# Attention and adapters on one core: the first q's path, the last batch's parts, PSUM at the end, the load depth and the engine of the relus

## The chip, the core and the metric

The kernel runs on one core of a Trainium2 chip. The metric is the device time of one execution in microseconds (us). Before the change, 13 executions took 198.45 to 203.11 us, with a median of 201.2 us.

Five engines of the core work side by side, each through its own instructions in order: TensorE (PE; its weight loads are shown apart as PEld), VectorE (DVE), ScalarE (ACT), GpSimd (POOL) and SyncE (SP). Here POOL issues the loads that change the type on the way, SP issues the rest. Matrix products land in PSUM, which has 8 banks of 512 f32 per partition; DVE and ACT bring them from there to SBUF.

## What is computed

```python
# q, k, v: (8, 12, 448, 64) f32; w_gate (768, 8); A (8, 768, 16); B (8, 16, 768)
scores = scale * np.matmul(q, k.transpose(0, 1, 3, 2))
attn = np.maximum(scores, 0.0) ** 2 / S
attn_out = np.matmul(attn, v)
x = attn_out.transpose(0, 2, 1, 3).reshape(B * S, H * D)      # 3584 x 768
logits = x @ w_gate
topk = np.argpartition(-logits, K, axis=1)[:, :K]             # K = 2 of 8 experts
w = softmax over the two chosen logits
out = x + sum over the two: w * ((x @ A[e]) @ B[e])
```

## The kernel before

**Attention.** A quad is four heads of one batch (two heads in each half of the 128 partitions); with three quads a batch there are 24 quads. Per quad, three loads (q, k, v, line 305) of two DMAs each are issued on POOL and change f32 to bf16. PE transposes q and k (56 products, line 397) into two PSUM banks, and DVE copies all of it to `qkT` (line 408). A step `n` is 64 keys (`j`, seven of them) against a part of the batch's queries: four 64x64 products give the scores in two PSUM banks (`qk`, line 427), ACT takes the relu with a scale into the tile `a1` (line 450), DVE squares two steps at a time into `a2` (line 464), and PE multiplies by v, accumulating over the seven `j` (`pv`, line 481). The result goes to the transposed activations `xt` by one ACT and one DVE copy (`xt_copy`, line 504). In seven batches a step has all 448 queries; the last batch is worked in two parts of 224 (`UB = [1] * (B - 1) + [2]`), so that there are 147 steps of 448 and 42 of 224.

**Adapters.** Tokens go in 28 tiles of 128 columns of `xt`, and gates in groups of up to three tiles (the last two groups have two). `gate` multiplies by `awg`, the adapters' A and the gate weights side by side (line 522), picks the two experts in a chain of small DVE and ACT operations (lines 539 to 579), and transposes the weighted result (line 599) to `zT` (line 611). `outputs` adds, for each tile, x itself by products with the identity (`f_id`, line 628) and two f32 products with B (`f_b`, line 644) in two PSUM banks, copied to `osb` by ACT (one half) and DVE (the other, line 663) and stored from SP (line 679) in pieces of neighbouring rows of the output. `awg` itself is put in order by 72 products (line 345).

**The order of the work** is made on the host, before the launch, by a list scheduler (`schedule`, line 56): each operation has the engines that may take it, an assumed duration and latency, dependences, a rank (its due step, plus a constant `D_...` for its kind), and what it takes of pools and PSUM banks. On each engine the runnable operation of the lowest rank goes next; on PE a change of mode adds `SWITCH` to the rank, and a `qk` is put ahead when the relus that ACT still has to do would run out (`cover`, line 116). `choose` (line 79) grants PSUM: up to three pairs of banks for scores (`SCAP`), one tile for outputs at a time (`"o": 1`), and at most two of the four pairs for anything but scores. The order that comes out is what each engine's queue then holds. A load of quad x + `AHEAD` becomes runnable when quad x has been transposed; the first `AHEAD` quads' loads are issued at the start, after the identity, in the order q, k, v, with `sel` and A behind the first three quads (lines 685 to 695). `pv` of a first `j` waits for the squares `DEFER` steps later.

Of the kernel before, what the change touches and what calls it, by code (L numbers as in the profile page):

```python
# [14 lines left out]
J = 7  # L15
PH = 64
PU = 32

SLACK = -0.162
SWITCH = 1.913  # L20
THIRD = 0.612
SCAP, MCAP, TCAP = 3, 2, 1
DEFER = 5
AHEAD = 5
# [31 lines left out]
def schedule(ops, switch=0.1, hop=0.05):  # L56
# [8 lines left out]
    relus = []  # L65
    seq = {id(o): i for i, o in enumerate(ops)}
# [12 lines left out]
    def choose(o):  # L79

        c, n = o.want
        if used[c] >= {"s": SCAP, "t": TCAP, "p": 2, "m": MCAP, "o": 1}[c]:
            return None
        slots = sorted((x for x in range(0, 8, 2) if x in freed and x + 1 in freed),
                       key=lambda x: max(freed[x], freed[x + 1]))
        if c == "s":
            if used["s"] >= 2 and any(
                x.want and x.kind != "qk" and x.ready <= t + 1e-9 and x.rank <= o.rank + THIRD
                for x in avail["PE"]
            ):  # L90
                return None
            return [slots[0], slots[0] + 1] if slots else None
        halves = sorted((x for x in freed if x ^ 1 not in freed), key=lambda x: freed[x])
        if n == 1 and halves:
            return halves[:1]
        busy = 4 - len(slots) - used["s"]
        if not slots or busy >= 2:
            return None

        if n == 1 and busy == 1 and any(  # L100
            x.want and x.ready <= t + 1e-9 and x.kind in ("pv", "tp") and x.rank <= o.rank
            for x in avail["PE"]
        ):
            return None
        return [slots[0], slots[0] + 1][:n]

    def pick(e):
        c = [o for o in avail[e] if can(o)]
        if not c:
            return None  # L110
        if e != "PE":
            return min(c, key=lambda o: (o.rank, seq[id(o)]))
        best = min(c, key=lambda o: (o.rank + SWITCH * (o.mode != mode), seq[id(o)]))
        if best.kind != "qk":

            cover = max(free["ACT"], t) + sum(o.dur["ACT"] for o in relus)
            q = [o for o in c if o.kind == "qk"]
            if q and t + best.dur[e] + 0.1 * (best.mode != mode) + 0.1 * (best.mode != "64") + 0.4 > cover + SLACK:
                return q[0]
        return best  # L120

    left = len(ops)
    while left:
# [9 lines left out]
        for e in free:  # L133
# [42 lines left out]
            events.append(free[e])  # L176
            order.append(o)
# [18 lines left out]
def kernel(  # L196
# [51 lines left out]
    UB = [1] * (B - 1) + [2]  # L248

    D_QK = -3.314  # L250
    D_SQ = 6.0
    D_PV = 1.585
    D_XT = 3.031
    D_TP = -12.164
    D_TPE = -1.578
    D_Z = 0.984
    D_GATE = -2.244
    D_ZT = 12.0
    D_ZTE = 5.985
    D_ID = 9.569  # L260
    D_OUT = 13.172
# [3 lines left out]

    make_identity(nc, identf)
    nc.vector.tensor_copy(identb, identf)
# [23 lines left out]
    RELU = {448: 0.80, 224: 0.424}  # L291

# [7 lines left out]
    def load(b, w, c, deps):  # L300
        def fn():
            nm = f"{'qkv'[w]}n{c}"
            T[b, w, c] = loads.tile([128, 2, J * Dh], BF16, name=f"{nm}_{b}", tag=nm)
            for g in range(2):
                nc.gpsimd.dma_start(  # L305
                    out=T[b, w, c][g * PH : g * PH + PH],
                    in_=(qv, kv, vv)[w][b, g, :, 2 * c : 2 * c + 2, :],
                )


        return op(("POOL",), 1.3, 2.0, fn, deps=deps, kind="load")
# [24 lines left out]
    def aw_place(half, deps):  # L336

        d0 = half * 3

        def mm():  # L340
            for x in range(3):
                for i in range(DO):
                    y0 = 128 * (d0 + x) - i + DO - 1
                    for rhs, lo, hi in ((a_raw[:, :, i, :], 0, RE), (g_raw[:, i, :], RE, ZW)):
                        nc.tensor.matmul(  # L345
                            out=bank(m)[:, x * ZW + lo : x * ZW + hi],
                            lhsT=sel[:, y0 : y0 + 128],
                            rhs=rhs,
                            start=(i == 0 and lo == 0),
                            stop=(i == DO - 1),  # L350
                            skip_group_check=True,
                        )

        def ev():
            nc.vector.tensor_copy(
                awg[:, d0 : d0 + 3, :], bank(m)[:, : 3 * ZW].rearrange("p (x w) -> p x w", x=3)
            )

        m = op(PE, 18 * 0.085, PL, mm, deps=deps, mode="128", kind="fill", banks=("m", 1))
        return op(DVE, dve(3 * ZW), DL, ev, deps=[m], free=[(m, 0)], rank=-20.0)  # L360


    def width(b):
        return S // UB[b]

    order = []
    for b in range(B):
        if UB[b] == 1:
            order += [(b, 0, c, j) for c in range(NC_) for j in range(J)]
        else:  # L370
            order += [(b, u, c, j) for u in range(UB[b]) for c in range(NC_) for j in range(J)]
# [8 lines left out]
    while n < NS:  # L380
        m = 2 if n + 1 < NS and width(order[n][0]) == width(order[n + 1][0]) else 1
        for i in range(m):
            pair_of[n + i] = (n, m, i)
        n += m

    loaded, tp_ops = {}, {}
    qk_ops, relu_ops, sq_ops, pv_ops, xt_ops = {}, {}, {}, {}, {}

    def tp(b, c):
# [16 lines left out]
        def ev():  # L406
# [6 lines left out]
        m = op(PE, 2 * TPD, PL, mm, deps=[loaded[b, 0, c], loaded[b, 1, c]], mode="64", kind="tp",  # L413
               banks=("t", 2), take=("qkT",), rank=first_use[b, c] + D_TP)
        return op(DVE, dve(4 * J * PH, 1.92), DL, ev, deps=[m], free=[(m, 0)], rank=m.rank + D_TPE)

    def qk(n):
        b, u, c, j = order[n]
        pu = PH // UB[b]

        def fn():
            qk_ = T["qkT", b, c]
            for sl in range(2):
                r0 = sl * PH
                x0 = 0 if sl else 512 - width(b)
                for a in range(2):
                    nc.tensor.matmul(  # L427
                        out=bank(o, sl)[a * PH : a * PH + PH, x0 : x0 + width(b)].rearrange(
                            "p (j s) -> p j s", j=J
                        ),  # L430
                        lhsT=qk_[r0 : r0 + PH, a, 1, j * PH : j * PH + PH],
                        rhs=qk_[r0 : r0 + PH, a, 0, :].rearrange("p (j s) -> p j s", j=J)[
                            :, :, u * pu : u * pu + pu
                        ],
                        start=True,
                        stop=True,
                    )

        o = op(PE, 0.194 / UB[b], PL, fn, mode="64", kind="qk", deps=[tp_ops[b, c]],
               after=qk_ops.get(n - 1), banks=("s", 2), give=("qkT",) if n == last_use[b, c] else (), rank=n + D_QK)  # L440
        return o

    def relu(n):
        W = width(order[n][0])
        g0, m, i = pair_of[n]

        def fn():
            if i == 0:
                new("a1", ("a1", g0), [128, m, 2 * W], BF16)
            nc.scalar.activation(T["a1", g0][:, i], both(qk_ops[n], W), ACTF.Relu, scale=relu_scale)  # L450

        return op(ACT, RELU[W], AL, fn, deps=[qk_ops[n]], after=relu_ops.get(n - 1), kind="relu",
                  take=("a1",) if i == 0 else (), free=[(qk_ops[n], 0)], rank=n)

    def sq(n):

        W = width(order[n][0])
# [13 lines left out]
    def pv(n):  # L471
        b, u, c, j = order[n]
        W = width(b)
# [16 lines left out]
        if j == 0:  # L490
            wait += [sq_ops[min(n + DEFER, NS - 1)]]
        o = op(PE, 0.194 / UB[b], PL, fn, mode="64", kind="pv", deps=wait, after=pv_ops.get(n - 1),
               banks=("p", 2) if j == 0 else None, give=("a2",) if i == m - 1 else (),
               rank=n - j + DEFER + D_PV)
# [3 lines left out]
    def xt_copy(n):  # L498
        b, u, c, j = order[n]
        W = width(b)  # L500
        col = b * S + u * W
# [10 lines left out]
    def gate(tiles_):  # L512
        v = tile_due[tiles_[0]]
# [103 lines left out]
    def outputs(tile_):  # L617
# [52 lines left out]
        def st():  # L670
            osb = T["osb", tile_]
            r = 0
            while r < 128:
                b, x = divmod(c0 + r, S)
                pu = PH // UB[b]
                u, y = divmod(x, J * pu)
                j, p = divmod(y, pu)
                m = min(pu - p, 128 - r)
                nc.sync.dma_start(out=outv[b, j, u * pu + p : u * pu + p + m], in_=osb[r : r + m, :])
# [4 lines left out]

    b_load = op(("SP",), 0.5, 3.0, b_fn, kind="load")
    op(("POOL",), 1.4, 0.0, lambda: None)
    def first_loads(x0, x1):
        for x in range(x0, x1):
            for w in range(3):
                loaded[x // NC_, w, x % NC_] = load(x // NC_, w, x % NC_, [])  # L690

    first_loads(0, NC_)
    sel_op = op(("POOL",), 1.5, 0.1, sel_fn)
    a_load = op(("POOL",), 2.0, 3.0, aw_fn, kind="load")
    first_loads(NC_, AHEAD)
# [10 lines left out]
    for tl in range(NT):  # L706
        x = 128 * tl + 127
        b2, y = divmod(x, S)
        own = max(n for n, (b, u, c, j) in enumerate(order) if b == b2 and u == y // width(b)) + DEFER + 2
        tile_due[tl] = max(own, tile_due.get(tl - 1, 0) + PACE)  # L710
# [4 lines left out]
    def finish(n):  # L715
# [6 lines left out]
        for tl in range(NT):  # L722
# [3 lines left out]
            for col in range(128 * tl, 128 * tl + 128, PU):  # L726
                b2, x = divmod(col, S)
                need |= {(b2, x // width(b2), c2) for c2 in range(NC_)}
# [59 lines left out]
```

## Time and profile before

| | |
|---|---|
| median of 13 executions | 201.2 us |
| the profiled execution's own time | 201.77 us |
| its span, first to last instruction | 199.9 us |
| mean granted TensorE clock | 0.988 |
| first products of scores; first relu | 9.45 us; 10.09 us |
| last relu begins; last product ends; last copy ends | 181.04; 195.1; 195.70 us |
| last load issue on POOL | 116.4 us |

The profile gives busy times by engine, by 40 slices of the span, and by groups of instructions (line, engine, operation, tiles and shapes, with the mean duration of one, and what ended the idle time before them). A trace answers further: a table of busy time in chosen stretches, the instructions of a stretch in order of time (start, duration, engine, line, what it writes and reads, how many), and the chain of waits, followed back from the last instruction. Products are pipelined, so that one that stands alone shows more time than its place in a dense row.

### The profile page before, as it was taken

The page shows a single profiled execution, that of the slowest core. Times are in us where ns is not written, and L with a number is a line of the kernel's source. Part 1 is how long each engine was busy: PE and PEld are TensorE (multiplying, and loading weights), DVE is VectorE, ACT ScalarE, POOL GpSimd, SP SyncE. Part 2 cuts the span into 40 slices and gives each one's busy share as a digit, 9 for nine tenths or more (in the row PEclk, how much of TensorE's full clock was granted, in tenths as well). Part 3 has the DMA queues.
Part 4 walks back from the last instruction along what each step waited for, and adds up shares of the span by engine and source line. Part 5 has one row for each costly group of instructions (what it writes and reads, how often), then busy time and mean ns, then how long its engine had stood idle before and what let it go on. Part 6 is the DMA issues. An engine that isn't in the chain of part 4 may idle for free.

```text
span 199.9 us, 8860 instructions
## 1 busy us (share of the span) xinstructions
PE 172.9 (87%) x3908; PEld 102.7 (51%) x3908; DVE 161.2 (81%) x285; ACT 166.7 (83%) x255; POOL 89.3 (45%) x154
## 2 busy tenths in 40 slices
PE   0498878868999998999589998999998999999990
PEld 0345756545464555456346554565544756655640
DVE  0269879999799889998499999999999887895521
ACT  2099988999999989999599999999998799794220
POOL 8999899896967784977442720000000000000000
PEclk9999996999999999999999999999999999999998
DMA  5999999999999999999969892312330333336676
GB/s 114 173 183 142 168 168 183 192 179 172 155 220 234 218 187 201 198 209 202 194 126 164 122 194 62 77 27 65 79 82 3 82 84 82 82 79 150 161 178 151
DMA packets 26694, 28.70 MB, mean 144 GB/s; under 512 B 4512, under 2 KB 22944, under 8 KB 26656
## 3 DMA queue, kind: packets, MB, share of 16 engines
q0 software_dynamic: 21920, 16.73, 58.7%
q1 hardware_dynamic: 4736, 11.41, 20.8%
q8 instruction: 30, 0.49, 1.0%
q14 instruction: 8, 0.07, 0.1%
HBM read 33.84 MB, written 11.01 MB: 224 GB/s over the span
## 4 chain that ended last, share of the span: by engine, by line
PE 55%; ACT 21%; DVE 12%; issue 6%; DMA 2%; POOL 1%; ACTq 0%; DVEq 0%; POOLq 0%
PE ps L644 19%; ACT a L450 18%; PE ps L481 13%; PE ps L427 11%; DVE qkT L408 5%; PE ps L397 4%; DVE a L464 4%; PE ps L628 3%; PE ps L522 3%; DMA kn<-in_k_dram 2%; ACT xt L504 2%; PE ps L345 2%; DVE osb L663 1%; POOL qn L305 1%; PE ps L599 0%
## 5 line engine op out<-in xcount | busy, mean ns | idle before, releaser
L450 ACT ACTIVATE a<-ps 128x896 bf16<-128x896 f32 (+1 forms) x189 | 148.1, 863 | 14.9 <-PE ps L427 14.2
L464 DVE TENSOR_TENSOR a<-a 128x1792 bf16<-128x1792 bf16 (+1 forms) x95 | 92.0, 980 | 8.6 <-ACT a L450 8.2
L427 PE MATMUL ps<-qkT 64*64 64x448 bf16 (+1 forms) x756 | 64.2, 353 | 7.0 <-ACT a L450 4.6
L644 PE MATMUL ps<-B_sb,zT 128*128 128x384 f32 x112 | 49.2, 532 | 0.4 <-DVE zT L611 0.4
L481 PE MATMUL ps<-a,vn 64*64 64x448 bf16 (+1 forms) x756 | 45.4, 339 | 2.7 <-ACT a L450 1.7
L427 PEld LDWEIGHTS <-qkT 64*64 64x64 bf16 x756 | 24.0, 107 | 40.5 <-issue 33.4
L408 DVE COPY qkT<-ps 128x1792 bf16<-128x1792 bf16 x24 | 26.1, 1089 | 13.0 <-PE ps L397 12.5
L305 POOL DMA_DIRECT2D vn<-in_v_dram x48 | 29.3, 630 | 14.5 <-PE ps L427 6.9
L305 POOL DMA_DIRECT2D kn<-in_k_dram x48 | 29.5, 633 | 6.8 <-DMA qn<-in_q_dram 4.1
L481 PEld LDWEIGHTS <-vn 64*64 64x64 bf16 x756 | 25.2, 108 | 13.9 <-issue 7.6
L305 POOL DMA_DIRECT2D qn<-in_q_dram x48 | 29.4, 631 | 5.1 <-DMA vn<-in_v_dram 4.6
L663 DVE COPY osb<-ps 128x384 f32<-128x384 f32 x28 | 15.5, 553 | 9.3 <-PE ps L644 9.2
L663 ACT COPY osb<-ps 128x384 f32<-128x384 f32 x28 | 14.3, 510 | 9.5 <-PE ps L644 7.2
L644 PEld LDWEIGHTS ps<-B_sb,zT 128*128 128x128 f32 x112 | 17.2, 188 | 7.9 <-issue 4.0
L397 PE MATMUL ps<-identb,qn 64*64 64x64 bf16 x672 | 10.6, 201 | 6.7 <-DMA qn<-in_q_dram 6.1
L397 PEld LDWEIGHTS <-qn 64*64 64x64 bf16 x672 | 10.3, 116 | 10.6 <-DMA qn<-in_q_dram 6.3
L504 DVE CAST xt<-ps 128x448 bf16<-128x448 f32 (+1 forms) x27 | 15.3, 567 | 0.5 <-PE ps L481 0.5
L397 PE MATMUL ps<-identb,kn 64*64 64x64 bf16 x672 | 12.1, 203 | 3.7 <-issue 3.3
L504 ACT CAST xt<-ps 128x448 bf16<-128x448 f32 (+1 forms) x27 | 13.8, 511 | 1.7 <-PE ps L481 1.7
L522 PE MATMUL ps<-awg,xt 128*128 128x136 bf16 x168 | 13.7, 224 | 0.5 <-DVE qkT L408 0.5
L522 PEld LDWEIGHTS <-xt 128*128 128x128 bf16 x168 | 10.2, 98 | 5.6 <-issue 5.0
L628 PEld LDWEIGHTS <-xt 64*64 64x64 bf16 x672 | 10.0, 108 | 5.3 <-issue 3.9
(30 smaller groups left out, 71.8 us busy)
## 6 DMA issues: line engine op xcount, KB each, us to landing
out_dram<-osb SPq DMA_DIRECT2D x49, 192.0 KB, 3.5
qn<-in_q_dram POOLq DMA_DIRECT2D x48, 112.0 KB, 4.9
kn<-in_k_dram POOLq DMA_DIRECT2D x48, 112.0 KB, 5.1
vn<-in_v_dram POOLq DMA_DIRECT2D x48, 112.0 KB, 4.8
out_dram<-osb SPq DMA_DIRECT2D x14, 96.0 KB, 1.9
B_sb<-in_moe_B_dram SPq DMA_DIRECT2D x1, 384.0 KB, 3.2
a_raw<-in_moe_A_dram POOLq DMA_DIRECT2D x1, 192.0 KB, 4.0
g_raw<-in_moe_w_gate_dram POOLq DMA_DIRECT2D x1, 12.0 KB, 3.3
```

Of the source, the lines that this page charges most:

```text
L305: nc.gpsimd.dma_start(out=T[b, w, c][g * PH : g * PH + PH], in_=(qv, kv, vv)[w][b, g, :, 2 * c : 2 * c + 2, :],)
L397: nc.tensor.transpose(ps_b[sl * PH : sl * PH + PH, m.banks[g], (w * J + j) * PH : (w * J + j) * PH + PH,], T[b, w, c][r, sl, j * Dh : j * ...
L408: nc.vector.tensor_copy(sb.rearrange("p g w x -> p g (w x)"), ps_b[:, m.banks[0] : m.banks[0] + 2, : 2 * J * PH],)
L427: nc.tensor.matmul(out=bank(o, sl)[a * PH : a * PH + PH, x0 : x0 + width(b)].rearrange("p (j s) -> p j s", j=J), lhsT=qk_[r0 : r0 + PH, a, ...
L450: nc.scalar.activation(T["a1", g0][:, i], both(qk_ops[n], W), ACTF.Relu, scale=relu_scale)
L464: nc.vector.tensor_mul(a2, T["a1", g0], T["a1", g0])
L481: nc.tensor.matmul(out=bank(head, g)[sl * PH : sl * PH + PH, :W], lhsT=vn[r0 : r0 + PH, sl, j * Dh : j * Dh + Dh], rhs=T["a2", g0][r0 : r0 ...
L504: evac(W, lambda cp, g=g: cp(xt[:, g * NC_ + c, col : col + W], bank(src, g)[:, :W]), engs=SETS[(E_X0, E_X1)[g]], deps=[pv_ops[n]], free=[ ...
L522: nc.tensor.matmul(out=z[:, t * ZW : t * ZW + ZW], lhsT=xt[:, do, 128 * tiles_[t] : 128 * tiles_[t] + 128], rhs=awg[:, do, :], start=(do = ...
L628: nc.tensor.matmul(out=bank(o_id, r)[tok * PH : tok * PH + PH, do * PH : do * PH + PH], lhsT=xt[rr, do, c0 + tok * PH : c0 + tok * PH + PH ...
L644: nc.tensor.matmul(out=bank(o_id, r)[:, : D // 2].rearrange("p (o d) -> p o d", o=DO), lhsT=T["zT", g0][:, zi * 128 : zi * 128 + 128], rhs ...
L663: cp(T["osb", tile_].rearrange("p (o r d) -> p r o d", r=2, d=PH)[:, r], bank(o_id, r)[:, : D // 2].rearrange("p (o d) -> p o d", o=DO),)
```

## The change

It has eight parts.

1. The first quad's q is loaded by two plain f32 DMAs, one from SP and one from ACT, into an own tile, and turned to bf16 by one cast on DVE and one on ACT (`load_q0`). On SP it goes ahead of B.
2. The first load on POOL is then k of quad 0, ahead of the identity, which becomes a scheduled operation; then q, k of quad 1, v of quad 0, and so on. `sel` and A stand behind the loads of the first three quads but one v.
3. The first quad's transposes are copied in three: q by DVE, the first 64 keys by ACT, the other keys by DVE. The first `qk` needs the first two only.
4. Relus may go to DVE (`RDN = 189`: all steps). DVE takes one only if ACT is busy for more than `BEHIND` = 0.596 us yet, and after its own work whose rank is less than the relu's plus `YIELD` = 2.
5. The last batch has parts of 46 and 18 of each 64 rows: 322 and 126 queries, 21 steps each. The last part's columns run in the order of the output's rows, so that its store is one DMA.
6. PSUM: outputs may hold two tiles (`OCAP`), and three once no `qk` is left, when all four pairs may be used by others than scores.
7. `AHEAD` goes from 5 to 3, `DEFER` from 5 to 4; the assumed time of a load on POOL from 1.3 to 1.55.
8. All rank constants change (`SWITCH` from 1.913 to 5.491 among them); the last `pv`s and the last gate are ranked earlier by `HURRY` = 4.782; the products of line 345 come in six pieces instead of two, with a rank of their own (`D_A` = 18).

```diff
-SLACK = -0.162
-SWITCH = 1.913
-THIRD = 0.612
+SLACK = -0.248
+SWITCH = 5.491
+RDN = 189
+BEHIND = 0.596
+YIELD = 2.0
+OCAP = 2
+THIRD = 6.193
-DEFER = 5
-AHEAD = 5
+DEFER = 4
+AHEAD = 3
...
-        if used[c] >= {"s": SCAP, "t": TCAP, "p": 2, "m": MCAP, "o": 1}[c]:
+        if used[c] >= {"s": SCAP, "t": TCAP, "p": 2, "m": MCAP, "o": OCAP if qks else 3}[c]:
...
-        if not slots or busy >= 2:
+        if not slots or busy >= (2 if qks else 4):
...
+        if e == "DVE":
+            r = [o for o in c if o.kind == "relu"]
+            if r and free["ACT"] <= t + BEHIND:
+                c = [o for o in c if o.kind != "relu"]
+            elif r:
+                c = [o for o in c if o.kind == "relu" or o.rank < r[0].rank + YIELD]
...
-            return min(c, key=lambda o: (o.rank, seq[id(o)]))
+            return min(c, key=lambda o: (o.kind == "relu" and e == "DVE", o.rank, seq[id(o)]))
...
-    UB = [1] * (B - 1) + [2]
+    PARTS = [[(0, PH)]] * (B - 1) + [[(0, 46), (46, PH)]]
...
-    make_identity(nc, identf)
-    nc.vector.tensor_copy(identb, identf)
...
+    def load_q0():
+        def fn():
+            T["q0"] = const.tile([128, 2, J * Dh], F32, name="q0")
+            for g, e in enumerate((nc.sync, nc.scalar)):
+                e.dma_start(out=T["q0"][g * PH : g * PH + PH], in_=qv[0, g, :, 0:2, :])
+        def cast(sl):
...
+            (nc.vector.tensor_copy, nc.scalar.copy)[sl](T[0, 0, 0][:, sl], T["q0"][:, sl])
...
+        if first:
+            oq = op(DVE, dve(2 * J * PH, 1.92), DL, lambda: part(nc.vector.tensor_copy, 0, 0, J * PH),
+                    deps=[m], rank=-30.0)
+            ok = op(ACT, act(2 * PH), AL, lambda: part(nc.scalar.copy, 1, 0, PH), deps=[m], rank=-30.0)
+            o = op(DVE, dve(2 * (J - 1) * PH, 1.92), DL, lambda: part(nc.vector.tensor_copy, 1, PH, J * PH),
+                   deps=[oq], free=[(m, 0)], rank=-30.0)
...
-            nc.scalar.activation(T["a1", g0][:, i], both(qk_ops[n], W), ACTF.Relu, scale=relu_scale)
...
+            if o.eng == "ACT":
+                nc.scalar.activation(T["a1", g0][:, i], both(qk_ops[n], W), ACTF.Relu, scale=relu_scale)
+            else:
+                nc.vector.tensor_scalar(
+                    T["a1", g0][:, i], both(qk_ops[n], W), relu_scale, 0.0, op0=ALU.mult, op1=ALU.max
+                )
...
+                b, u, y = part_at(c0 + r)
+                p0, p1 = PARTS[b][u]
+                if (b, u) == order[-1][:2]:
+                    m = 128 - r
+                    dst = out[b * S + J * p0 + y : b * S + J * p0 + y + m, :]
+                else:
+                    j, p = divmod(y, p1 - p0)
+                    m = min(p1 - p0 - p, 128 - r)
+                    dst = outv[b, j, p0 + p : p0 + p + m]
+                nc.sync.dma_start(out=dst, in_=osb[r : r + m, :])
...
+    loaded[0, 0, 0] = load_q0()
     b_load = op(("SP",), 0.5, 3.0, b_fn, kind="load")
...
+    first_load(0, 1)
+    o = op(("POOL",), 0.7, 0.0, ident_fn)
+    ident_op = op(DVE, 0.23, DL, lambda: nc.vector.tensor_copy(identb, identf), deps=[o], rank=-40.0)
+    for x in range(1, AHEAD):
+        first_load(x, 0)
+        first_load(x, 1)
+        first_load(x - 1, 2)
     sel_op = op(("POOL",), 1.5, 0.1, sel_fn)
     a_load = op(("POOL",), 2.0, 3.0, aw_fn, kind="load")
-    first_loads(NC_, AHEAD)
+    first_load(AHEAD - 1, 2)
```

## The prediction

> **What bounds the kernel now.** I read first the table of busy time by stretches, then the chain of waits, then single stretches in order of time. The table (columns: stretch and length; PE, PEld, DVE, ACT, POOL busy, with counts; granted clock; DMA share; GB/s):
>
> ```profile
> 9.45:20.00 10.55, 9.69 (x196) 5.19 (x197) 7.79 (x8) 9.86 (x13) 10.16 (x17) 1.00 1.25 164
> 20.00:40.00 20.00, 16.57 (x422) 12.02 (x422) 17.13 (x28) 18.17 (x26) 17.82 (x31) 0.91 1.19 178
> 40.00:60.00 20.00, 17.70 (x417) 10.21 (x417) 18.73 (x28) 19.89 (x27) 16.61 (x29) 1.00 1.16 181
> 60.00:80.00 20.00, 18.73 (x433) 10.83 (x436) 18.41 (x31) 19.43 (x30) 13.78 (x24) 1.00 1.18 210
> 80.00:100.00 20.00, 17.23 (x414) 9.87 (x404) 16.65 (x25) 17.66 (x25) 13.90 (x24) 1.00 1.15 201
> 100.00:120.00 20.00, 19.20 (x451) 11.04 (x449) 19.09 (x32) 19.84 (x29) 8.30 (x14) 1.00 0.85 152
> 120.00:140.00 20.00, 18.78 (x442) 10.77 (x435) 18.61 (x31) 19.93 (x29) 0.00 (x0) 1.00 0.23 57
> 140.00:160.00 20.00, 18.76 (x453) 11.01 (x449) 18.64 (x42) 18.13 (x32) 0.00 (x0) 1.00 0.24 61
> 160.00:195.10 35.10, 34.59 (x654) 20.60 (x652) 24.24 (x66) 22.48 (x53) 0.00 (x0) 1.00 0.48 117
> ```
>
> There are four stages. Until 9.45 us no scores are made. From there to 160 us ACT sets the pace (133.05 of 140 us after 20, against DVE 127.26 and PE 126.97: all three are nearly full, and ACT is the fullest). From 160 to 195.1 PE is full (34.59 of 35.1), working off outputs that were put back. The last 4.8 us are a copy and stores. Since the last stage is PE's backlog, I do the sum in PE's time: from 9.45 to 195.1 PE is idle 185.65 - 171.24 = 14.4 us, 13.9 of it before 160. The end moves by what PE starts earlier, idles less, or has less to do.
>
> The chain of waits shows the start and the two largest holes (start, length, what):
>
> ```profile
> 3.31 4.33 DMA kn<-in_k_dram
> 7.68 0.60 PE ps L397 x22
> 8.31 1.10 DVE qkT L408
> 9.45 0.61 PE ps L427 x4
> 10.09 0.77 ACT a L450
> ...
> 27.87 1.21 issue
> ...
> 95.03 2.07 issue
> ```
>
> The start is k's second DMA, third to last of what POOL issues up to it: identity, two DMAs of q, two of k.
>
> **Part 1 to 3, the start.** POOL's q issue (1.33 us for two) goes away and the identity moves behind k, so k's first issue stands at the 0.74 us at which POOL's first own instruction stands now, its second about 0.66 later, at 1.40, and lands 4.33 later, at 5.7 instead of 7.64. q must not be later: B's plain DMA of 384 KB from SP is issued at 0.74 and lands in 3.2, so q's halves (224 KB f32 each) land by 4.0 if ACT issues at once, by 5.3 if its DMA stands behind the table load (0.74 to 2.02). A cast of 448 elements is bounded by the PSUM casts of that shape (0.62 DVE, 0.56 ACT) and by the 0.23 of the identity's: q is ready at 4.5 to 5.9. The identity, moved past one load, is made by about 2.7 and cast by 3.0: hidden, 2 us to spare. So after k's landing: k's 28 transposes 0.6 (6.3), the ACT copy of 128 elements (0.35, the 224-element cast, as upper bound) instead of DVE's 1.10 (6.7), scores to relu 0.64 as now: first relu at 7.3, gain 2.8. If q is last (5.9, then q and k transposes 0.9 together): 7.8, gain 2.3. If three streams at once slow k by a further 1 us, gain 1.8. I take **-2.6** (-1.6 to -3.2). It lasts only if the next quads keep up: POOL's order k0, identity, q1, k1 puts k1's last issue at about 4.4 and its landing (5.1 median for k) at 9.5; four relus from 7.3 last to 10.6, so transposes and copy of quad 1 just about fit. v0 goes from fifth to eighth pair of places, issued by 6.3, landing by 11.1; the first `pv` now starts at 16.73, so that is covered. B, moved behind q on SP by 0.4 us, is used at 48.7.
>
> Here the Trainium skill speaks against the change: its page SBUF — State Buffer, "SBUF: two separate sides", holds that an f32 SBUF copy on VectorE shuts GpSimd out from writing descriptors while it runs. By it the DVE cast of q would put one load issue back by less than a microsecond; no run here shows such a cast yet.
>
> **Part 7, AHEAD and DEFER.** POOL and the DMA queues are fullest early: the DMA share is 1.15 to 1.25 until 100 us, 0.24 once loads end at 116. Both holes above are PE waiting for nothing recorded in the middle of a row of transposes, and ACT then starves (0.65 and 2.31 us of idle). That they lie only where loads are dense is correlation, not cause. With three quads ahead the loads run some two quads (two of 6.6 us) longer, to about 130, at 95/110 of the density. I price the holes at half gone: **-1.5** (0 to -3.3). Their cover: three quads are about 20 us of lead against 5 of landing; should transposes wait, one quad's wait is a load's landing less what is queued, at most 5 us once. DEFER only reorders: 0.
>
> **Part 4, relus on DVE.** A relu on ACT takes 0.82 in a dense row (4.15 for five). DVE has no such row; its PSUM reads of 448 elements to bf16 take 0.618 and of 384 f32 0.553, 1.02 ns an element, so 896 take 0.618 + 448 x 1.02 ns = 1.07. Each moved relu frees 0.82 on ACT and costs 1.07 on DVE. Queued behind it there: squares, copies of `qkT`, `xt` and gates, each later by up to 1.07. Over 20 to 160, 133.05 - 0.82k = 127.26 + 1.07k at k = 3, both 130.5: so ACT and DVE alone would permit 9 us less, PE with 127 a little more. But packing three engines at 97% isn't to be had: of the 10.6 us that PE idles before 160 besides the holes (13.9 - 3.3), I take 4 as regained: **-4** (0 to -8; above zero see the first rival).
>
> **Parts 6 and 8, PSUM and ranks.** A tile's two B products take 1.49 in one run (157.73) and 0.84 each when scores come between, and a lone score of four takes 0.32 against 0.19 in a row: some 0.2 lost per interleaving, on 21 of the 28 tiles. A larger SWITCH and two output tiles in PSUM join some: -1 (0 to -4). At the end PE's only wait is 0.45 (190.8 to 191.7, for the last zT), so all PSUM for outputs buys at most that: -0.3. The pieces of line 345 keep their 3.2 us.
>
> **Part 5, the last batch.** Columns stay 448, instructions too. A group of four products takes 0.19 at 448 and about 0.095 at 224 (16 in 0.38): 0.137 at 322 by the line between. At 126 the line gives 0.053, the weight loads' pace (28 in 0.62) 0.089; I take 0.089. Then 42 x (0.137 + 0.089 - 0.19) = **+1.5** (0 to +3, if the strided reading of the last part costs as much again). Relus are linear (0.16 + 0.74 ns an element from the 0.82 and 0.49 rows): no change. Only one tile, not two, then hangs on the last part; its gate chain, from first product (186.29) to B product (191.74), is 5.45 us and now nearly all under two other tiles' outputs (187.1 to 190.8). If that cover is gone it costs 3.5 us more.
>
> The last stores now take 4.2 us from the last copy (195.70 to 199.9). The last tile will have two pieces (2 and 126 rows) instead of several of 32, so the last issue comes 0.9 earlier (two issues of 0.47 fewer), but moves 378 KB: landing 1.9 for 96 KB, 3.5 for 192 KB, so 3 to 5. I take 0 (-1.5 to +2.5).
>
> Against part 5 stands also a rule of the Trainium skill, DMA: Bandwidth & Descriptors, "Why a DMA increments its semaphore by 16 and not by 1": a transfer spreads over the largest number of engines up to 16 that divides its rows, so pieces of 46 rows would go over two engines, 126 rows over 14. No store before has such a row count; by it the 46-row pieces would hold `osb` buffers longer.
>
> **Sum.** -2.6 - 1.5 - 4 - 1 - 0.3 + 1.5 + 0 = -7.9: the span goes to 192.0. The profiled execution's time is 201.77 for 199.9, so 193.9; it lies 0.57 over the median, so against that **193.5 us**.
>
> **Rivals.** A measurement here tells 1% from nothing, so faster means under 199.2, slower over 203.2.
>
> *DVE becomes the bound (slower).* The rule lets DVE take a relu whenever it comes free in the first 0.2 us of one on ACT, and puts squares behind it unless they lag four steps. DVE has 12.7 us free in the 140. With 1.07 each that is 12 relus; at 20 the DVE stretch is 8.7 over, less 2.6 at the start: about +6, 206. It decides from 15 relus up (15 x 1.07 - 12.7 = 3.3, more than the start brings). For it: squares feed PE and are served late, and `a1` has four buffers only. Against it: a full DVE doesn't come free early, so the number limits itself. The same price covers a schedule whose assumed times miss the chip's. 0.19.
>
> *Only the start counts (a little faster).* Holes stay, PE's idle time stays since QK waits for PSUM, the last batch's +1.5 eats a part: -2.6 + 1.5 - 0.5 = -1.6, 199.6. 0.15.
>
> *PE's row order fails (no change).* The last gate's cover is lost (+3.5) and the start's gain with it: 202. 0.06.
>
> **How the numbers follow.** The forecast holds with 0.60; its own range is 189.5 to 198. The lower end is the sum with the ends of parts 4 and 7 (-5.8 more) held back by what PE can do; the upper takes the start and half of part 4. To leave no more than two in ten out, the range goes to 189 and to 202, past the second rival and the third. Faster: 0.60 and a third of the second rival's 0.15, plus 0.03 of less likely sizes, 0.68. Same: 0.13. Slower: 0.19.
>
> **What would show it.** First relu near 7.3; the largest "issue" pieces in the chain below 1 us; DVE relus of 1.07, fewer than 15; PE idle from its first scores to its last product near 8; more B products in fours; scores of 126 columns in a pitch of 0.09. I'm wrong if squares wait behind relus so that PE idles over 14 us, if transposes of early quads wait for loads, or if PE's total work grows by over 3 us.

## The result, and the profile after

The change made the kernel slower: 210.88 us (median of 11 executions, 209.86 to 213.17) against 201.72 us (48 executions), a ratio of 1.053 (95% interval 1.050 to 1.056). Ratios leave out the executions that lie over 1.5% above the fastest of their kernel and medians don't, so that a ratio isn't the quotient of two medians. I had predicted 193.5 us and a range of 189 to 202. The profiled execution after has a span of 209.0 us, 9.1 more than before.

The table of busy time by stretches, for the changed kernel up to its last products (columns as in the prediction):

```profile
9.75:20.00 10.25, 8.80 (x196) 4.87 (x196) 9.12 (x9) 9.35 (x12) 9.61 (x16) 1.00 1.16 149
20.00:40.00 20.00, 17.52 (x430) 11.04 (x426) 19.75 (x31) 18.16 (x26) 17.42 (x30) 1.00 1.15 166
...
80.00:100.00 20.00, 19.64 (x444) 11.11 (x444) 18.99 (x32) 19.53 (x29) 13.65 (x23) 1.00 1.17 209
...
160.00:194.50 34.50, 33.26 (x583) 18.50 (x579) 21.07 (x63) 18.33 (x48) 0.00 (x0) 1.00 0.39 98
```

Up to here nothing was lost. PE is busier than before in nearly every stretch (131.6 us of the 140 from 20 to 160, where it was 127.0), the hole at 95 us is gone, and the last copy ends at 194.01 instead of 195.70. So the 9.1 us come after the last computation. The same table for the end, where after the last copy the engines stand still and only the DMA share and its GB/s (the last two columns) say anything, first for the old kernel, whose last copy ends at 195.70:

```profile
194.00:196.00 2.00, 1.10 (x4) 0.35 (x2) 0.56 (x1) 0.48 (x1) 0.00 (x0) 1.00 0.83 194
196.00:198.00 2.00, 0.00 (x0) 0.00 (x0) 0.00 (x0) 0.00 (x0) 0.00 (x0) 1.00 0.85 201
198.00:200.00 2.00, 0.00 (x0) 0.00 (x0) 0.00 (x0) 0.00 (x0) 0.00 (x0) 0.61 0.22 52
```

Then for the changed one:

```profile
194.00:196.00 2.00, 0.00 (x0) 0.00 (x0) 0.01 (x1) 0.00 (x0) 0.00 (x0) 1.00 0.12 43
196.00:198.00 2.00, 0.00 (x0) 0.00 (x0) 0.00 (x0) 0.00 (x0) 0.00 (x0) 0.51 0.49 134
198.00:200.00 2.00, 0.00 (x0) 0.00 (x0) 0.00 (x0) 0.00 (x0) 0.00 (x0) 0.50 0.60 192
200.00:202.00 2.00, 0.00 (x0) 0.00 (x0) 0.00 (x0) 0.00 (x0) 0.00 (x0) 0.50 0.13 49
...
204.00:206.00 2.00, 0.00 (x0) 0.00 (x0) 0.00 (x0) 0.00 (x0) 0.00 (x0) 0.50 0.13 52
206.00:208.00 2.00, 0.00 (x0) 0.00 (x0) 0.00 (x0) 0.00 (x0) 0.00 (x0) 0.50 0.09 35
```

From the last copy to the end the old kernel took 4.2 us, the new one 15.0. From 200 to about 207 us the DMA share stands at 0.13, which is two of sixteen engines, at about 50 GB/s. Among the DMA issues there are row counts that no store had before (KB each; the old kernel's stores were of 192 and 96 KB, 64 and 32 rows):

```profile
out_dram<-osb SPq DMA_DIRECT2D x4, 138.0 KB
...
out_dram<-osb SPq DMA_DIRECT2D x1, 378.0 KB
```

138 KB are 46 rows of 3 KB, 378 KB are 126 rows.

The start brought nothing either. The chain of waits of the changed kernel (start, length, what):

```profile
1.95 6.15 DMA kn<-in_k_dram
...
8.77 0.64 DVE qkT L460
...
9.43 0.28 ACT qkT L460
...
9.75 0.59 PE ps L493 x4
```

k's second DMA is issued 1.4 us earlier than before, but it is under way for 6.15 us instead of 4.33, and the first relu begins at 10.39 instead of 10.09. That place varies from run to run: in six profiles with this start (this one, and five of the runs below) it lies between 10.03 and 10.89, with the old start in two at 10.09 and 10.66.

### The profile page after: what moved, and what is told of

It reads as the page before. It is cut to its first block, busy times and chain, and to the rows that moved or that the text cites. A ratio compares the mean times of both kernels' runs of the same rounds, so it can differ in the third digit from the quotient of the medians.

```text
span 209.0 us, 8868 instructions
## 1 busy us (share of the span) xinstructions
PE 175.1 (84%) x3908; PEld 101.9 (49%) x3908; DVE 164.8 (79%) x291; ACT 165.1 (79%) x254; POOL 88.1 (42%) x152
## 4 chain that ended last, share of the span: by engine, by line
PE 52%; DVE 17%; ACT 15%; issue 5%; DMA 3%; POOL 0%; ACTq 0%; DVEq 0%; POOLq 0%
PE ps L716 19%; PE ps L493 14%; ACT a L517 13%; PE ps L553 8%; DVE a L536 6%; DVE qkT L452 6%; PE ps L441 4%; PE ps L594 4%; PE ps L700 3%; DMA kn<-in_k_dram 3%; ACT xt L576 1%; DVE osb L735 1%; DVE a L519 1%; DVE xt L576 1%; PE ps L671 1%
## 5 line engine op out<-in xcount | busy, mean ns | idle before, releaser
L517 ACT ACTIVATE a<-ps 128x896 bf16<-128x896 f32 (+2 forms) x186 | 146.1, 858 | 11.1 <-PE ps L493 9.6
L536 DVE TENSOR_TENSOR a<-a 128x1792 bf16<-128x1792 bf16 (+3 forms) x96 | 92.5, 974 | 7.5 <-ACT a L517 7.1
L493 PE MATMUL ps<-qkT 64*64 64x448 bf16 (+2 forms) x756 | 70.3, 376 | 7.6 <-ACT a L517 3.5
L493 PEld LDWEIGHTS <-qkT 64*64 64x64 bf16 x756 | 26.2, 107 | 45.5 <-issue 34.0
L553 PE MATMUL ps<-a,vn 64*64 64x448 bf16 (+2 forms) x756 | 45.8, 331 | 2.0 <-DVE qkT L452 0.7
L320 POOL DMA_DIRECT2D qn<-in_q_dram x46 | 28.0, 625 | 5.4 <-DMA vn<-in_v_dram 4.3
L452 DVE COPY qkT<-ps 128x1792 bf16<-128x1792 bf16 x23 | 25.0, 1088 | 1.6 <-PE ps L441 0.8
L441 PE MATMUL ps<-identb,qn 64*64 64x64 bf16 x672 | 10.7, 199 | 7.8 <-DVE qn L338 6.0
L576 DVE CAST xt<-ps 128x448 bf16<-128x448 f32 (+2 forms) x27 | 15.3, 568 | 1.0 <-PE ps L553 0.9
L576 ACT CAST xt<-ps 128x448 bf16<-128x448 f32 (+2 forms) x27 | 14.0, 517 | 0.7 <-PE ps L553 0.7
L594 PE MATMUL ps<-awg,xt 128*128 128x136 bf16 x168 | 13.4, 224 | 0.0
L441 PE MATMUL ps<-identb,kn 64*64 64x64 bf16 x672 | 11.3, 201 | 0.4 <-issue 0.2
## 6 DMA issues: line engine op xcount, KB each, us to landing
out_dram<-osb SPq DMA_DIRECT2D x49, 192.0 KB
```

The costliest lines, as they stand in the source:

```text
L320: nc.gpsimd.dma_start(out=T[b, w, c][g * PH : g * PH + PH], in_=(qv, kv, vv)[w][b, g, :, 2 * c : 2 * c + 2, :],)
L441: nc.tensor.transpose(ps_b[sl * PH : sl * PH + PH, m.banks[g], (w * J + j) * PH : (w * J + j) * PH + PH,], T[b, w, c][r, sl, j * Dh : j * ...
L452: nc.vector.tensor_copy(sb.rearrange("p g w x -> p g (w x)"), ps_b[:, m.banks[0] : m.banks[0] + 2, : 2 * J * PH],)
L493: nc.tensor.matmul(out=cols(bank(o, sl)[a * PH : a * PH + PH, x0 : x0 + W]), lhsT=qk_[r0 : r0 + PH, a, 1, j * PH : j * PH + PH], rhs=(qk_[ ...
L536: nc.vector.tensor_mul(a2, T["a1", g0], T["a1", g0])
L553: nc.tensor.matmul(out=bank(head, g)[sl * PH : sl * PH + PH, :W], lhsT=vn[r0 : r0 + PH, sl, j * Dh : j * Dh + Dh], rhs=T["a2", g0][r0 : r0 ...
```

## The experiments

### The end: which store lasts

One edit in how the last batch's rows are cut for the store; the order of work on every engine stays the same.

```diff
                     m = min(p1 - p0 - p, 128 - r)
+                    if m in (46, 38):
+                        m = 32
```

> The changed kernel with one edit in the stores: pieces of 46 and 38 rows go as 32 rows and the rest (14 or 6); all else, the order on every engine included, stays. Theory A (such pieces run over two of the sixteen DMA engines, as their row counts divide by no larger number up to 16): the stretch at some 50 GB/s after the last copy (194.0 to about 207.5 us) goes, the last copy stays at 194 +-1, the span ends at 198 to 199.5, a time of about 200.5 to 201.5 (ratio to before 0.99 to 1.00). Rival B (one store of 378 KB at the very end is what lasts): the tail stays over 13 us, time 209 to 212. Rival C (more DMA issues on SP cost as much): time 203 to 206.

Measured: 201.88 us, a ratio of 1.003 (0.999 to 1.007), a little over the 200.5 to 201.5 expected. The last copy ends at 194.44, the span at 200.2. The end of that run by stretches:

```profile
194.00:196.00 2.00, 0.00 (x0) 0.00 (x0) 0.44 (x1) 0.00 (x0) 0.00 (x0) 1.00 0.60 145
196.00:198.00 2.00, 0.00 (x0) 0.00 (x0) 0.00 (x0) 0.00 (x0) 0.00 (x0) 0.92 0.72 235
198.00:200.00 2.00, 0.00 (x0) 0.00 (x0) 0.00 (x0) 0.00 (x0) 0.00 (x0) 0.50 0.10 38
```

The stretch at a share of 0.13 is gone though five more DMAs are issued. The other cut leaves those pieces and splits the largest store:

```diff
                     m = 128 - r
+                    if m == 126:
+                        m = 112
```

> The changed kernel with the last store of 126 rows cut to 112 and 14; the pieces of 46 and 38 rows stay. Theory A: nothing moves, 210 to 212, the tail at some 50 GB/s stays to about 207. Rival B: the tail falls to 5 to 7 us, time 201 to 203.

Measured: 210.84 us, ratio 1.050 (1.042 to 1.057), span 208.3. Nothing moved beyond the interval, so it isn't the size of the last store. The opposite test puts a bad row count into the old kernel, in its very last tile:

```diff
                 m = min(pu - p, 128 - r)
+                if tile_ == NT - 1 and m == 32:
+                    m = 31
```

> The kernel before the change with one edit: the four store pieces of 32 rows of the very last tile go as 31 and 1 rows. Theory A (a piece goes over as many of the sixteen DMA engines as the largest number up to 16 that divides its rows: one engine for 31) gives 4 x 93 KB through one engine at some 25 GB/s, half of the 51 GB/s seen for two: about 15 us instead of 4.2 after the last copy, a span near 211, at a DMA share of 0.06 and 25 GB/s. Rival H (only the total of bytes and issues counts): four more issues of 0.5 on SP, span 201 to 203.

Measured once: 218.12 us, a span of 216.1 with the last copy at 197.04: 19.1 us of stores alone, more than the 15 expected. That the one engine first has its share of the tiles before to finish would fit; no run shows it apart. Its end by stretches:

```profile
200.00:205.00 5.00, 0.00 (x0) 0.00 (x0) 0.00 (x0) 0.00 (x0) 0.00 (x0) 0.50 0.06 24
205.00:210.00 5.00, 0.00 (x0) 0.00 (x0) 0.00 (x0) 0.00 (x0) 0.00 (x0) 0.50 0.07 26
210.00:214.00 4.00, 0.00 (x0) 0.00 (x0) 0.00 (x0) 0.00 (x0) 0.00 (x0) 0.50 0.06 26
```

A share of 0.06 is one engine of sixteen, at 25 GB/s: half of what pieces of 46 and 38 rows reached. This is the rule of the Trainium skill that the prediction cited (DMA: Bandwidth & Descriptors, "Why a DMA increments its semaphore by 16 and not by 1"): 46 and 38 divide by 2 and by nothing else up to 16, 31 by 1 only. The runs agree with it. In numbers of these runs: four pieces of 46 rows and one of 38 are 222 rows of 3072 bytes, 0.68 MB; at 51 GB/s that is 13.4 us, if all of it went over the same two engines. The first such issue stands at 189.1 us, so this alone would end at 202.5 and not at 207; the two engines' share of the other stores would come on top, which no run shows apart.

Then the remedy that costs no DMA: parts whose rows divide by 16.

```diff
-    PARTS = [[(0, PH)]] * (B - 1) + [[(0, 46), (46, PH)]]
+    PARTS = [[(0, PH)]] * (B - 1) + [[(0, 48), (48, PH)]]
```

> The changed kernel with the last batch in parts of 48 and 16 of each 64 rows (336 and 112 queries): every store piece is then a multiple of 16 rows; the last part's columns still run in the output's row order. Theory A: tail from the last copy 4 to 5 us, time 200 to 201.5, like the run with split pieces or some 0.3 better (fewer issues). Rival B: the last store is 336 KB, a tail of over 12 us, 208 or more.

Measured: 200.89 us, ratio 0.996 (0.992 to 1.001), last copy at 194.81, span 199.1. Its end by stretches:

```profile
194.00:196.00 2.00, 0.21 (x1) 0.00 (x0) 0.56 (x1) 0.13 (x1) 0.00 (x0) 1.00 0.77 209
196.00:198.00 2.00, 0.00 (x0) 0.00 (x0) 0.00 (x0) 0.00 (x0) 0.00 (x0) 1.00 0.58 177
```

These pieces are no smaller than those of 46 rows, and no stretch at 0.13 is left. So the store's row counts are all of the 5% that the runs can tell; what is left of the change is worth nothing measurable.

### The last batch: reading the queries 64 apart

```diff
-        rows = (b, u) == order[-1][:2]
+        rows = False
...
-                if (b, u) == order[-1][:2]:
+                if False:
                     m = 128 - r
```

> As the run with parts of 48 and 16 rows, but the last part's columns run as in all other parts (seven runs of 16 neighbouring columns) so that PE reads its queries in runs and not 64 elements apart; its store becomes seven pieces of 16 rows. Theory D (the strided reading costs PE: two groups of scores of 126 columns took 0.66 us against 0.39 of 224): the 84 products of scores fall from a pitch of about 0.25 per group of four to 0.1, the last product ends 2 to 3 us earlier, seven store issues of 0.5 take up to 2 of it back: time 0.5 to 2.5 under the row-order run. Rival E (scores there wait for ACT's relus anyway, the width is modelled time): equal or up to 2 slower for the stores.

Measured: 200.08 us, ratio 0.998 (0.993 to 1.002). Groups of instructions by shape: the narrow scores of the run with rows in the output's order, then of this one (products, busy us, mean ns):

```profile
L493 PE MATMUL ps<-qkT 64*64 64x112 bf16 x84 | 7.1, 381 | 0.1
```

```profile
L493 PE MATMUL ps<-qkT 64*64 64x112 bf16 x84 | 3.8, 219 | 0.3 <-ACT a L517 0.3
```

Theory D holds for PE: the same 84 products take 3.3 us less when their queries lie in runs. The last copy came 1.5 earlier (193.33), but the tail grew from 4.3 to 6.2 us with seven pieces instead of one. In time the two runs are the same within their intervals.

### The start: two late arrivals that hide each other

Three runs on the kernel with parts of 48 and 16. First the activation table:

```diff
                 e.dma_start(out=T["q0"][g * PH : g * PH + PH], in_=qv[0, g, :, 0:2, :])
+            warm = const.tile([128, 1], F32, name="warm")
+            nc.vector.memset(warm, 0.0)
+            nc.scalar.activation(warm, warm, ACTF.Relu)
```

> The run with parts of 48 and 16 rows, and besides a one-element activation on ACT right behind its q issue, so that the activation table is loaded while q is under way (there it ran from 5.50 to 6.78, after ACT's wait for q). Theory F (the start is lost to that table load in front of ACT's cast): ACT's cast of q ends near 6.1 instead of 7.35, first relu 10.03 -> 9.0 to 9.4 if k has landed by then. Theory G (k itself lands late, since q and B move beside it): first relu stays at 9.7 to 10.1. Time 0 to 1 us under the parts-48 run.

Measured: 200.45 us, ratio 0.996 (0.993 to 0.999), as without the edit. The chain of waits:

```profile
1.95 6.49 DMA kn<-in_k_dram
...
8.49 0.60 PE ps L444 x22
```

ACT's cast of q ended at 5.93 instead of 7.35, and the first relu still came at 10.73: k landed at 8.44. Then B alone:

```diff
-        nc.sync.dma_start(out=B_sb, in_=moe_B.rearrange("e r d -> (e r) d"))
+        nc.gpsimd.dma_start(out=B_sb, in_=moe_B.rearrange("e r d -> (e r) d"))
...
-    b_load = op(("SP",), 0.5, 3.0, b_fn, kind="load")
...
     first_load(AHEAD - 1, 2)
+    b_load = op(("POOL",), 0.7, 3.0, b_fn, kind="load")
```

> The run with parts of 48 and 16 rows, with B's 384 KB issued on POOL behind the first three quads' loads instead of on SP right behind q. Theory G: q lands near 4.5 (5.5 there), k by 7, first relu 9.0 to 9.4. Theory F: q's cast on ACT still follows its landing by 1.3 for the table, first relu falls by the earlier landing of q alone, 9.0 to 9.5 as well, but k's transposes then wait for q's, not for k. If neither: 10.0. Time 0 to 1 us under the parts-48 run.

Measured: 201.15 us, ratio 0.998 (0.994 to 1.001), first relu at 9.88. The expectation of 9.0 to 9.4 was too good: q landed only 0.2 earlier, and 9.88 is hardly outside the 10.03 to 10.89 of the start without the edit. Instructions in order of time:

```profile
5.34 1.28 ACT L338 ACT_TABLE_LOAD   x1 [5.34 <-DMA q<-in_q_dram]
...
6.64 0.56 ACT L338 CAST qn<-q 128x448 bf16<-128x448 f32 x1
...
7.61 0.60 PE L441 MATMUL ps<-identb,kn 64*64 64x64 bf16 x28
```

Now k's transposes wait for no DMA, but they stand behind q's, and q's behind the table load that ACT begins only once q is there. The third run has both edits, and takes the last part's scores in runs of 16 columns, put in the output's order by the copies to `xt`, so that one store of 112 rows is left:

```diff
-        rows = (b, u) == order[-1][:2]
+        rows = False
...
-            evac(W, lambda cp, g=g: cp(xt[:, g * NC_ + c, col : col + W], bank(src, g)[:, :W]),
+            evac(W, lambda cp, g=g: cp(out_cols(xt[:, g * NC_ + c, col : col + W]), in_cols(bank(src, g)[:, :W])),
```

(For the last part both functions turn `p (s j)` and `p (j s)` to `p j s`; for others they change nothing.)

> The run with parts of 48 and 16 rows, with the early table load, B behind on POOL, and the last part's scores in runs of 16 columns as in the key-major run, put in the output's row order by the copies to xt (so one store of 112 rows). If F and G both hold: first relu 8.0 to 8.8; the 84 products of the narrow scores take 3.8 us busy as in the key-major run instead of 7.1; last copy near 191.5 to 193, tail 4.3: a time 2 to 4 us under the parts-48 run, so 197 to 199.

Measured in four executions: 199.52 us, ratio 0.983 (0.974 to 0.992), first relu at 8.44. Too few executions for so small an effect, so once more:

> The kernel of the start-and-columns run once more, in more rounds, since that one was timed only four times (ratio 0.974 to 0.992). First relu near 8.4, tail 4.3: if the gain is real the ratio to before is 0.980 to 0.992 (197 to 199.5 us); if it was a lucky draw, 0.993 to 1.00.

Measured in 12: 198.22 us, ratio 0.9875 (0.9835 to 0.9915). This kernel is faster than both, by some 1.2% than the one before the change; what of that is the start and what the columns, no run takes apart. Its span is 195.8, its last copy at 191.54. Its start in order of time:

```profile
1.49 1.28 ACT L336 ACT_TABLE_LOAD   x1 [1.49 <-PEq L862]
...
5.66 0.56 ACT L341 CAST qn<-q 128x448 bf16<-128x448 f32 x1 [2.67 <-DMA q<-in_q_dram]
...
6.75 0.56 PE L444 MATMUL ps<-identb,kn 64*64 64x64 bf16 x28
...
8.99 2.53 ACT L520 ACTIVATE a<-ps 128x896 bf16<-128x896 f32 x3 [0.69 <-PE ps L496]
```

With both out of the way the first relu begins at 8.4 to 9.0 (8.44, 8.99, and 8.42 and 8.62 in the two runs below, which have the same start), where one edit alone left it at 9.9 or 10.7. q itself now ends the wait: 4.84 us under way. The time from issue to landing of k's two first DMAs (shortest, median and longest), with B on SP in the changed kernel, then here:

```profile
DMA to landing us min/median/max: 4.7/5.4/6.1
```

```profile
DMA to landing us min/median/max: 4.2/4.4/4.7
```

Over all profiles the longer of the two took 5.5 to 6.65 us in the seven with B on SP and 4.0 to 4.7 in the five with B behind, beside the same two loads of q. So theory G holds, and it is B, beside q's loads, that slows k.

### Relus on DVE, loads ahead, PSUM

Without any relu on DVE (`RDN = 0`), on the kernel with parts of 48 and 16:

> The run with parts of 48 and 16 rows, with RDN = 0: no relu on DVE (three there, at 11.0, 16 and 29 us). My prediction's step (relus on DVE regain 4 us of PE's idle time) would make this run 3 to 5 us slower than the parts-48 run; since there are only three such relus, 2.5 us of ACT's work, I now expect within 1.5 us of it, with PE's idle time up by no more than that.

Measured: 200.73 us, ratio 0.999 (0.995 to 1.003), against 0.996 (0.992 to 1.001) with them: not to be told apart. The changed kernel has three relus on DVE, of 1.09 us each, all begun before 30 us. The 140 us in the middle (PE busy first), with the relus on DVE and without:

```profile
20.00:160.00 140.00, 130.03 (x3045) 76.86 (x3044) 132.17 (x215) 134.45 (x191) 69.79 (x118) 1.00 0.85 150
```

```profile
20.00:160.00 140.00, 130.15 (x3054) 76.21 (x3050) 130.99 (x213) 136.79 (x195) 71.92 (x122) 1.00 0.87 151
```

The last two are edits of the best kernel, in one session with it. `AHEAD = 5`:

> The start-and-columns kernel with AHEAD = 5 as before the change: two quads more are loaded at the start. My prediction's step (three quads ahead thin the loads and halve the holes, worth 1.5 us) makes it 1 to 2 us slower than the same kernel with 3, with waits of PE in rows of transposes of 1 to 2 us again. But the changed kernel's last load was issued at 113.5 us, the old one's at 115.2: the loads were not thinned; then it is within 1 us, either way.

Measured: 199.52 us, ratio 0.9961 (0.9928 to 0.9995) against 0.9875 (0.9835 to 0.9915): slower by some 0.9%, 1.3 us in the medians. My expectation (within 1 us) was missed, and the prediction's size of 1.5 us fits. Its mechanism doesn't: the last two issues of loads begin at 112.2 us here and at 113.2 with three quads ahead, so the loads are not thinner. PE had done 128.2 us of work between 20 and 160 us, not 131.4. Which of its small waits make that up stays open, and so does whether the depth itself does it: the edit gives the host's scheduler another order for all engines (five relus on DVE instead of three), and the fit of the size may be luck.

The old PSUM rules:

```diff
-        if used[c] >= {"s": SCAP, "t": TCAP, "p": 2, "m": MCAP, "o": OCAP if qks else 3}[c]:
+        if used[c] >= {"s": SCAP, "t": TCAP, "p": 2, "m": MCAP, "o": 1}[c]:
...
-        if not slots or busy >= (2 if qks else 4):
+        if not slots or busy >= 2:
```

> The start-and-columns kernel with the PSUM rules as before the change (one output tile, two of four pairs to others than scores, also at the end). My prediction gave these rules and SWITCH together 1.3 us. The traces show no more B products in fours after the change than before (five against seven), so I now expect within 1 us of the same kernel with them; if the rules do carry the end, the last copy moves from 193.5 to 195 or later.

Measured: 198.60 us, ratio 0.992 (0.988 to 0.996), 0.4 us from the same kernel with the new rules, and the intervals overlap. Its one profile has the last copy 2.4 us later, but the times don't carry that; nothing is shown either way.

## Why the prediction was wrong, point by point

**Part 5, the last stores: the step that failed.** I took 0 (-1.5 to +2.5) for the time after the last copy, from the rows of 96 and 192 KB landing in 1.9 and 3.5 us, as if the price of a store went by its bytes. It was +10.8 (4.2 to 15.0), and that alone makes the change slower: without it the change is at 0.996 to 1.003 of the time before. Both rows were of 32 and 64 rows, and so said nothing of 46. I did quote the rule that bears on it, and drew from it that `osb` buffers would be held longer. That looks for the harm at the next user of a buffer; but nobody uses the last buffers again, and what waits there is the end of the program. The prediction's own rows give a price: once the loads end, 61 GB/s at a DMA share of 0.24 is some 16 GB/s an engine, so 0.68 MB over two engines would be some 21 us by that estimate, too much, but far beyond +2.5.

**The rest of the sum.** The forecast of the span was 192.0, it came at 209.0. Of the 17.0 us between, 6.2 lie ahead of the last product, which ended 1.7 us earlier (193.4 instead of 195.1) and not 7.9. In the sum's terms: PE's first scores came 0.3 later instead of 2.6 earlier; its idle time from there to the last product fell by 4.4 us (14.4 to 10.0) instead of 5.8 (parts 4 and 7 and the wait at the end); its work grew by 2.4 us (171.24 to 173.67) instead of 0.5 (+1.5 of part 5, -1 of parts 6 and 8). So the failed step explains the sign, and the parts below why so little was gained without it.

**Part 5, the narrow scores.** I took +1.5 for scores and `pv` of the last batch together. They went from 16.0 us busy to 20.2, so +4.2, past my upper end of 3: the strided reading cost about 3.3 of it, going by the runs with 112 columns (the changed kernel has 126), while `pv` of narrow parts cost almost nothing (5.9 before, 6.2 after).

**Parts 1 to 3, the start.** -2.6 was forecast, +0.3 came in this profile, -0.1 to +0.8 in all six. The case I had listed ("three streams at once slow k") came in at 1.2 to 2.3 us over the old 4.33 instead of 1, and by the runs with B behind it is B's doing. q, which I had landing by 4.0 or 5.3, landed at 5.5: its 224 KB took about 4.7 us. The table load that I had placed at 0.74 came behind ACT's wait for q, at 5.54, ahead of the cast; I had considered it only ahead of q. Each hid the other. The split copy saved little: ACT's 0.27 for 64 keys didn't run beside DVE's 0.62 of q, but after it.

**Part 4, relus on DVE.** -4 was forecast by balancing ACT against DVE at three moved relus. The count agrees (three), but by luck: they were of the first 30 us and no balance over 140, and taking them out changed nothing that could be measured. PE's idle time between 20 and 160 us did fall from 13.0 to 8.4 us by the change, but on the kernel with parts of 48 it is 10.0 with those relus and 9.9 without: they aren't its cause. What remains is the other order of work, which no run took apart.

**Part 7, loads ahead.** The size fits a later run (1.3 us between 5 and 3 quads in the best kernel); the reason given, thinner loads until 130 us, is refuted: loads ended at 114.7 us instead of 116.4. The two holes of PE in a row of transposes are gone from the profile after the change, but one of 1.2 us stands at 40.6 in the run with parts of 48, and one of 0.9 at 53.2 in the key-major run. In the old kernel they stood at the same places in two profiles (27.9 and 95.0; 29.6 and 96.5 in the run with 31-row pieces), so they seem tied to its order of instructions. Each of the four began 0.1 to 1.1 us after one of the 30 packets that the queue named "instruction" moves in a run; most of these packets have no such hole beside them, so this is a lead, and what PE waited for there no run shows.

**Parts 6 and 8.** -1.3 was forecast. B products in an unbroken four, each a tile's two halves, were seven before the change and five after it: the `qk` that keeps ACT supplied still comes between. Taking the PSUM rules back moved nothing that the times can tell; the rank constants were not tried apart.

**The rivals.** The slower one, DVE as the bound, didn't happen: DVE has 133.4 us of work in the 140 there and holds PE up there for 0.7 us at most at a time (1.4 us once before it, at 13.6). "Only the start counts" was turned round: the start brought nothing, the order in the middle a little. The last gate kept its cover: PE is busy without a break from 185 us to its last product.

## What to carry to other kernels

When a change alters how rows are cut for a store, look at the row count, not at the bytes: here pieces of 46 rows left a stretch with two DMA engines at work, pieces of 31 rows one with a single engine, and pieces of 48 none. Price a slower store twice, for the buffer's next user and for the end of the program, where nothing covers it. At the start, two arrivals that end within a microsecond of each other have to be moved together: against the 10.03 of the run with parts of 48, one edit alone brought 0.15 us at the first relu and the other none, both together 1.0 to 1.6.

## What was not expected of the hardware

- Scores of 112 columns whose queries were read 64 elements apart took 7.1 us for 84 products, in runs of 16 columns 3.8.
- The longer of k's first two loads of 112 KB on POOL's queue took 5.5 to 6.65 us beside two plain loads of 224 KB and B (384 KB), and 4.0 to 4.7 beside the two loads of 224 KB alone. In the old kernel the later of the two took 4.33, issued at 3.31, with B landed at 3.9.
- ACT's table load comes ahead of its first activation, but not always ahead of that one's wait: at 0.74 us before (the activation, a relu, began at 10.09), at 5.54 after, once q's DMA had landed, and at 1.49 with a one-element activation ahead of that wait. What decides on the side of the wait no run shows.
- The Trainium skill's page SBUF — State Buffer, "SBUF: two separate sides", holds that GpSimd can't write descriptors while VectorE runs a copy of f32 within SBUF in a mode that takes both ports, and the prediction took the cast of q for one. Here two issues beside that cast (0.39 us) took 1.24 us, their neighbours 1.21 to 1.22: no wait can be seen at this length. The cast itself took 0.39 to 0.41 us in nine profiles and 0.51 to 0.63 in three; what held it there no run shows.
